# Eight weight slots made 32 bytes longer each

## The chip, the cores and the metric

The kernel runs on one core of one Trainium2 chip. The metric is the device time of one execution in microseconds; of the kernel before there are three such times, and the median counts. Engines are TensorE (PE in the profile, its weight loads PEld), VectorE (DVE), ScalarE (ACT), GpSimd (POOL) and SyncE (SP).

## The reference

For each of four batches of 6080 rows and 256 columns, q and k are divided by the norms of their columns, their 256x256 product is put through a softmax, and v is multiplied with the result. All 24320 rows then go through a feed-forward layer whose activation is a ratio of polynomials.

```python
qn = q / (np.linalg.norm(q, axis=1, keepdims=True) + 1e-06)
kn = k / (np.linalg.norm(k, axis=1, keepdims=True) + 1e-06)
s = kn.transpose(0, 2, 1) @ qn / tau
a = softmax(s)                      # along the last axis
x = (v @ a).reshape(B * N, 256)
h = x @ w_in                        # 256 -> 2048
P = a0 + a1 * h + a2 * h**2 + a3 * h**3
Q = 1.0 + abs(b0) * abs(h) + abs(b1) * h**2
out = (P / (Q + 1e-06)) @ w_out     # 2048 -> 256
```

## The kernel before

**What it computes in which order.** For each batch the 256x256 softmax is multiplied into w_in, so that h comes straight from v: h = v @ (a @ w_in). This product is made in eight pieces of 256 columns (`fuse`, line 860), one for each p from 0 to 7. Each piece is kept as two tiles whose sum is the weight: the high half `whi`, a rounded copy (fp32r) that ScalarE writes, in the tag `w`, and the rest `wlo`, which VectorE writes, in the tag `w2`. There are eight slots of each, w0 to w7 and w20 to w27, and piece p of every batch lies in slot p. They are written once for each batch.

The rows of v are taken in 48 groups, eleven of 512 rows and one of 448 for each batch. `values` (line 889) brings v with channels on the partitions and splits it in the same manner, into `vhi` and `vlo`. For each group and each p, `pair` (line 941) does this:

- first product, into the PSUM tile `hx`: two halves i of 128 columns of h. For each half there are six matmuls (`mm1`, line 958), for each of the two 128-channel parts e: whi with vhi, whi with vlo, wlo with vhi. The weights are a 128x128 block of the tile, 512 bytes on each partition, and the stream is 512 (or 448) rows of v, 2048 (or 1792) bytes. The profile calls the first and the third `hx<-vhi,w` and the second `hx<-vlo,w`: it leaves out the numbers of buffers, so both `w` and `w2` read as w.
- the rational function on ScalarE, VectorE and GpSimd, which gives its value in two parts, `gh` and `gl`;
- second product, into `acc`: for each half gh with w_out_hi, gh with w_out_lo, gl with w_out_hi, two matmuls each.

So a pair has 24 matmuls of 512 columns, with a weight load before each, and there are 384 pairs.

**What sets the order.** A planner written into the kernel puts all steps in an order by costs and due times from tables, before the program is built. Each engine then works through its own list; semaphores tell it when data are there. Addresses play no part in it.

**Where tiles lie.** The pools have one buffer for each tile, laid one behind another in the order in which the loop over `homes` (lines 1140 to 1146) makes them, each start rounded up to 32 bytes. From that follow the starts on each partition, in bytes:

| tiles | start, before | residue of 128 | residue of 512 |
|---|---|---|---|
| ones | 17024 | 0 | 128 |
| w_in, w_out_hi, w_out_lo | 17888, 34272, 50656 | 96 | 480 |
| d, uu, r, kq, sq, orow | 67040 to 128480 | 96 | 480 |
| w0 to w7 | 132832 + 2048 each | 96 | 224 |
| w20 to w27 | 149216 + 2048 each | 96 | 224 |
| vst, vhi, vlo, sacc, ssq, gh, gl | 165600 to 208608 | 96 | 224 |

The blocks of 128 columns within a tile are 512 bytes apart and the two parts e of vhi, vlo, gh and gl 2048, so they all begin at the residue of their tile.

Of the kernel before, what the change touches and what calls it, by code (L numbers as in the profile page):

```python
# [10 lines left out]
F32 = mybir.dt.float32  # L11
# [286 lines left out]
def tile_channel_attention_rational_ffn(  # L298
# [15 lines left out]
    P = 128  # L314
# [51 lines left out]
    homes = {}  # L366
# [773 lines left out]
    for tag, width in homes.items():  # L1140
        if tag in ("hA", "hB"):
            continue
        home, n = (ps, SLOTS["hA" if tag == "hx" else tag]) if tag in ("hx", "acc") else (sb, SLOTS[tag])
        if tag == "n2":
            width += 16
        homes[tag] = [home.tile([P, width], F32, name=f"{tag}{i}") for i in range(n)]
    for s in plans[0][1]:
        s.fn()
# [39 lines left out]
```

## Time and profile before

| | |
|---|---|
| three runs | 2393.72, 2396.09, 2396.17 us; median 2396.09 |
| profiled execution | 2392.04 us, of which the span from first to last instruction is 2390.1 |
| PE busy | 2333.6 us (98%), 10312 matmuls |
| PEld busy | 1936.2 us (81%) |
| DVE, ACT, POOL busy | 2151.3, 2062.4, 1836.2 us (90, 86, 77%) |
| mean granted TensorE clock | 0.992 |

Times in the rows are microseconds from the start of the span unless marked ns. A busy TensorE means that some matmul is in flight; the end of a matmul is modelled, and each overlaps the next (389 ns long, 227 ns from start to start). How fast the matmuls follow one another is therefore read from start times, or from the chain of waits, where a row gives the time that a number of them took one after another.

### The profile page before, as it was taken

The numbers are of one execution on the slowest core, as the hardware profiler recorded it, in microseconds if no ns is written. First come the engines' busy times: TensorE is split into PE (matmuls) and PEld (weight loads), VectorE is DVE, ScalarE is ACT, GpSimd is POOL, SyncE is SP. The second block draws the span as 40 slices with busy tenths as digits, with TensorE's granted clock in tenths as the row PEclk, the third lists the DMA queues.
The fourth block names the chain that finished last, engine by engine and source line by source line (L and its number), as shares of the span: only waits on it lengthen the run. The fifth ranks groups of instructions, "written<-read, shape, count | busy, mean of one in ns | idle before, by whom it ended". The sixth has DMA issues, their size and how long they took to land.

```text
span 2390.1 us, 30382 instructions
## 1 busy us (share of the span) xinstructions
PE 2333.6 (98%) x10312; PEld 1936.2 (81%) x10312; DVE 2151.3 (90%) x2627; ACT 2062.4 (86%) x2072; POOL 1836.2 (77%) x1427
## 2 busy tenths in 40 slices
PE   7899999999999999999999999999998999999998
PEld 6688888888888888888888888888887788888887
DVE  5889999997878899999987889999996999999998
ACT  4789999987767799999986789999997999999996
POOL 7798777779779977777768987777774777777775
PEclk8999999999999999999999999999999999999999
DMA  9532121136467611211136731211111121111201
GB/s 298 160 77 36 18 36 18 18 58 150 88 141 156 122 26 20 34 19 26 27 83 146 162 72 20 34 19 27 26 19 18 19 35 18 27 28 18 33 11 19
DMA packets 455862, 141.15 MB, mean 59 GB/s; under 512 B 395888, under 2 KB 445040, under 8 KB 455696
## 3 DMA queue, kind: packets, MB, share of 16 engines
q1 hardware_dynamic: 447152, 108.04, 21.9%
q0 software_dynamic: 8544, 31.07, 7.3%
q8 instruction: 83, 1.36, 0.2%
q14 instruction: 83, 0.68, 0.1%
HBM read 83.10 MB, written 24.90 MB: 45 GB/s over the span
## 4 chain that ended last, share of the span: by engine, by line
PE 67%; ACT 15%; DVE 10%; issue 5%; DMA 1%; POOL 1%; SPq 0%; DVEq 0%; POOLq 0%; ACTq 0%
PE hx L83 37%; PE acc L83 30%; ACT d L83 6%; ACT r L83 5%; DVE hx L83 4%; ACT uu L83 3%; DVE gh L83 2%; DVE orow L83 2%; DVE gl L83 1%; POOL d L83 1%; DMA r<-in_q_dram 0%; DMA out_dram<-orow 0%; ACT L83 0%; DMA kq<-in_q_dram 0%; DMA d<-in_moe_w_in_dram 0%
## 5 line engine op out<-in xcount | busy, mean ns | idle before, releaser
L83 POOL TENSOR_TENSOR d<-d,gh 128x512 f32<-128x512 f32 (+1 forms) x768 | 978.6, 1303 | 411.1 <-DVE gh L83 407.1
L83 PE MATMUL hx<-vhi,w 128*128 128x512 f32 (+1 forms) x3072 | 1045.5, 389 | 5.1 <-DVE gl L83 4.1
L83 PEld LDWEIGHTS hx<-vhi,w 128*128 128x128 f32 x3072 | 577.1, 188 | 125.6 <-DVE gl L83 8.7
L83 DVE SCALAR_TENSOR_TENSOR hx<-hx,fast,d 128x512 f32<-128x512 f32 (+1 forms) x768 | 566.4, 745 | 60.4 <-POOL d L83 59.9
L83 PE MATMUL hx<-vlo,w 128*128 128x512 f32 (+1 forms) x1536 | 595.4, 388 | 0.0
L83 ACT ACTIVATE uu<-hx,fast 128x1024 f32<-128x1024 f32 (+1 forms) x384 | 422.3, 1100 | 148.9 <-PE hx L83 148.9
L83 DVE TENSOR_TENSOR gl<-hx,r 128x512 fp32r<-128x512 f32 (+1 forms) x768 | 518.1, 678 | 31.9 <-PE acc L83 4.8
L83 POOL TENSOR_SCALAR d<-d,ones,fast 128x1024 f32<-128x1024 f32 (+1 forms) x384 | 466.2, 1217 | 93.0 <-ACT r L83 89.9
L83 DVE SCALAR_TENSOR_TENSOR gh<-hx,fast,r 128x1024 fp32r<-128x1024 f32 (+1 forms) x384 | 485.5, 1265 | 43.6 <-ACT r L83 34.2
L83 DVE SCALAR_TENSOR_TENSOR hx<-uu,fast,hx 128x1024 f32<-128x1024 f32 (+1 forms) x384 | 487.4, 1269 | 32.3 <-ACT d L83 17.3
L83 PE MATMUL acc<-gh,w_out_hi 128*128 128x512 f32 (+1 forms) x1536 | 478.7, 393 | 14.2 <-DVE orow L83 10.8
L83 PE MATMUL acc<-gl,w_out_hi 128*128 128x512 f32 (+1 forms) x1536 | 472.6, 389 | 1.8 <-DVE gl L83 1.8
L83 PE MATMUL acc<-gh,w_out_lo 128*128 128x512 f32 (+1 forms) x1536 | 470.7, 388 | 0.0
L83 ACT ACTIVATE r<-d,fast 128x1024 f32<-128x1024 f32 (+1 forms) x384 | 439.0, 1144 | 11.1
L83 ACT ACTIVATE d<-hx 128x1024 f32<-128x1024 f32 (+1 forms) x384 | 386.7, 1007 | 63.1 <-PE hx L83 54.9
L83 ACT ACTIVATE r<-r 128x1024 f32<-128x1024 f32 (+1 forms) x384 | 403.0, 1050 | 8.3
L83 ACT ACTIVATE d<-d 128x1024 f32<-128x1024 f32 (+1 forms) x384 | 403.3, 1051 | 7.1
L83 PEld LDWEIGHTS acc<-gh,w_out_hi 128*128 128x128 f32 x1536 | 285.4, 188 | 82.1 <-DVE orow L83 25.1
L83 PEld LDWEIGHTS acc<-gl,w_out_hi 128*128 128x128 f32 x1536 | 287.9, 188 | 60.8 <-DVE gl L83 3.7
L83 PEld LDWEIGHTS acc<-gh,w_out_lo 128*128 128x128 f32 x1536 | 288.3, 188 | 57.8
L83 PEld LDWEIGHTS hx<-vlo,w 128*128 128x128 f32 x1536 | 288.7, 188 | 56.6
L83 PE MATMUL hx<-kq 128*128 128x256 f32 (+1 forms) x592 | 138.1, 388 | 11.6 <-DVE fast L83 6.8
(118 smaller groups left out, 1119.3 us busy)
## 6 DMA issues: line engine op xcount, KB each, us to landing
ssq<-sq POOLq DMA_DIRECT2D x54, 512.0 KB, 5.3
vst<-in_v_dram SPq DMA_DIRECT2D x176, 128.0 KB, 4.1
out_dram<-orow SPq DMA_DIRECT2D x176, 128.0 KB, 3.3
kq<-in_k_dram SPq DMA_DIRECT2D x75, 256.0 KB, 4.1
kq<-in_q_dram SPq DMA_DIRECT2D x75, 256.0 KB, 4.6
d<-in_moe_w_in_dram SPq DMA_DIRECT2D x8, 512.0 KB, 5.2
ssq<-sq POOLq DMA_DIRECT2D x6, 448.0 KB, 5.3
r<-in_k_dram SPq DMA_DIRECT2D x9, 256.0 KB, 5.4
```

Of the source, the lines that this page charges most:

```text
L83: ins = op(*args, **kwargs)
```

## The change

The slots of the tag `w` alone are made with eight more float32 each, 2080 bytes in place of 2048, and used through a view of the first 2048. No instruction changes its operation, shape or place in the order.

```diff
         if tag == "n2":
             width += 16
+        if tag == "w":
+            homes[tag] = [home.tile([P, width + 8], F32, name=f"{tag}{i}")[:, :width] for i in range(n)]
+            continue
         homes[tag] = [home.tile([P, width], F32, name=f"{tag}{i}") for i in range(n)]
```

The starts are then:

| tiles | start, after | residue of 128 | residue of 512 |
|---|---|---|---|
| w0, w1, w2, w3 | 132832, 134912, 136992, 139072 | 96, 0, 32, 64 | 224, 256, 288, 320 |
| w4, w5, w6, w7 | 141152, 143232, 145312, 147392 | 96, 0, 32, 64 | 352, 384, 416, 448 |
| w20 to w27 | 149472 + 2048 each | 96 | 480 |
| vst, vhi, vlo, sacc, ssq, gh, gl | 165856 to 208864 | 96 | 480 |

All tiles made before w0 stay where they were; all those behind w7 lie 256 bytes further on.

## Rows read from the trace of the kernel before

**Rows 1.** Granted clock: span and mean share of TensorE's full clock.

```profile
core 0: 2390.1 us, clock 0.992
```

**Rows 2.** The page: busy time of each engine, and the chain that ended last.

```profile
PE 2333.6 (98%) x10312; PEld 1936.2 (81%) x10312; DVE 2151.3 (90%) x2627; ACT 2062.4 (86%) x2072; POOL 1836.2 (77%) x1427
...
PE 67%; ACT 15%; DVE 10%; issue 5%; DMA 1%; POOL 1%; SPq 0%; DVEq 0%; POOLq 0%; ACTq 0%
PE hx L83 37%; PE acc L83 30%; ACT d L83 6%; ACT r L83 5%; DVE hx L83 4%; ACT uu L83 3%; DVE gh L83 2%; DVE orow L83 2%; DVE gl L83 1%; POOL d L83 1%; DMA r<-in_q_dram 0%; DMA out_dram<-orow 0%; ACT L83 0%; DMA kq<-in_q_dram 0%; DMA d<-in_moe_w_in_dram 0%
```

**Rows 3.** Busy time by stretch: engines with instruction counts, granted clock, DMA share.

```profile
100.00:500.00 400.00, 395.98 (x1732) 323.75 (x1731) 376.44 (x443) 373.44 (x365) 318.39 (x242) 1.00 0.22 41
500.00:1000.00 500.00, 497.54 (x2228) 416.75 (x2227) 428.49 (x526) 402.25 (x408) 405.92 (x316) 1.00 0.44 91
1000.00:1500.00 500.00, 497.69 (x2224) 415.55 (x2223) 445.65 (x544) 423.32 (x427) 396.35 (x310) 1.00 0.36 70
```

**Rows 4.** Chain from 1000 to 1100 us: start, time, and how many matmuls.

```profile
1002.30 5.44 PE acc L83 x24
1007.74 2.73 PE hx L83 x12
```

**Rows 5.** TensorE in order of time: a float32 product of k and q.

```profile
730.50 3.61 PE L83 MATMUL hx<-kq 128*128 128x256 f32 x16
```

**Rows 6.** Groups by line: first-product loads and writers of w, busy us, mean ns.

```profile
L83 PEld LDWEIGHTS hx<-vhi,w 128*128 128x128 f32 x3072 | 577.1, 188 | 125.6 <-DVE gl L83 8.7
...
L83 PEld LDWEIGHTS hx<-vlo,w 128*128 128x128 f32 x1536 | 288.7, 188 | 56.6
...
L83 DVE TENSOR_TENSOR w<-hx,w 128x512 fp32r<-128x512 f32 x32 | 21.9, 688 | 17.1 <-ACT w L83 17.0
...
L83 ACT ACTIVATE w<-hx 128x512 fp32r<-128x512 f32 x32 | 18.9, 595 | 30.7 <-PE hx L83 26.8 <-DVE hx L83 3.9
```

**Rows 7.** TensorE around 632 and 1222 us: small matmuls, weights from ssq and from ones.

```profile
632.38 0.95 PE L83 MATMUL hx<-ones,ssq 128*128 128x1 f32 x8
...
1222.25 0.61 PE L83 MATMUL hx<-kq,ones 128*128 128x128 f32 x4
1222.61 0.45 PE L83 MATMUL acc<-gl,w_out_hi 128*128 128x448 f32 x1
```

**Rows 8.** Matmuls, then loads, around 220 us: the second load of a pair is late.

```profile
219.77 0.39 PE L83 MATMUL hx<-vlo,w 128*128 128x512 f32 x1
...
221.13 0.39 PE L83 MATMUL hx<-vlo,w 128*128 128x512 f32 x1
...
219.77 0.46 PEld L83 LDWEIGHTS hx<-vhi,w 128*128 128x128 f32 x2
...
220.45 0.41 PEld L83 LDWEIGHTS hx<-vhi,w 128*128 128x128 f32 x2
```

**Rows 9.** Loads, then matmuls, around 572 us: the same, and what follows.

```profile
571.92 0.47 PEld L83 LDWEIGHTS hx<-vhi,w 128*128 128x128 f32 x2
...
572.14 0.62 PE L83 MATMUL hx<-vhi,w 128*128 128x512 f32 x2
...
573.76 0.62 PE L83 MATMUL acc<-gh,w_out_hi 128*128 128x512 f32 x2
```

**Rows 10.** TensorE: two rows of six 448-column matmuls, and what follows the first.

```profile
615.46 0.36 PE L83 MATMUL hx<-vhi,w 128*128 128x448 f32 x1
...
616.67 0.62 PE L83 MATMUL acc<-gh,w_out_hi 128*128 128x512 f32 x2
...
618.05 0.36 PE L83 MATMUL hx<-vhi,w 128*128 128x448 f32 x1
...
634.84 0.37 PE L83 MATMUL hx<-vhi,w 128*128 128x448 f32 x1
...
636.08 0.57 PE L83 MATMUL acc<-gl,w_out_hi 128*128 128x448 f32 x2
```

## The prediction

> **What bounds the kernel now.** I read the clock of the core first, then the busy times of the page, then the same by stage, then the chain that ended last, and only then single stretches of TensorE. [...] TensorE has an instruction in flight for 2333.6 of 2390.1 us [rows 2]; the stage table shows 395.98 of 400 us, then 497.5 and 497.7 of 500 [rows 3]. A busy share says little of how tightly matmuls follow one another, so the chain is the better witness: 67% of it is TensorE, 37% on the first product (hx) and 30% on the second (acc), and ScalarE and VectorE hold another 25% [rows 2]. So a gain on TensorE reaches the end only in part (I take its share of the chain, two thirds), a loss nearly in full.
>
> The chain also gives the pace. Twenty-four second-product matmuls of 512 columns take 5.44 us, that is 226.7 ns from one to the next, and twelve first-product ones take 2.73 us, 227 ns [rows 4]. Both products run at one pace, although the eight weight tiles of the first, the streamed vhi and vlo and the second product's gh and gl were laid out in other places than w_out_hi and w_out_lo. [...]
>
> **The change part by part.** No instruction is added, removed or moved; every queue has the same rows in the same order. What differs is addresses.
>
> The eight slots w0 to w7 hold the high halves of the fused weights. All began at residue 96 of 128 bytes, as w_out, w2, vhi, vlo, gh and gl do. Now w0 and w4 stay at 96, w1 and w5 begin at 0, w2 and w6 (the slots, not the w2 tiles) at 32, w3 and w7 at 64. A 128-column block of them is 512 bytes, so every load from a slot begins at the slot's residue. Eight times 32 is 256, so all that lies behind moves by 256 bytes and keeps its residue. Before, the first product had weights and stream at the same residue of 512 (224 and 224), the second at different ones (480 and 224), and the pace was the same 227 ns [rows 4]; so I cost the move by 256 at nothing.
>
> The writers: ScalarE writes the slots 32 times in all (18.9 us) and VectorE reads them back 32 times (21.9 us) [rows 6]. Even a tenth more on both would be 4 us, beside TensorE, on engines that are idle for 240 us and more of the span [rows 2]; I take 0, with 0 to 2 us for the range.
>
> The loads: of 4608 first-product loads (3072 with vhi, 1536 with vlo) [rows 6] two in three read a w slot (the third product, with vhi, reads w2), 3072, and six slots in eight have a new residue: **2304 loads**. Their own length is shown as 188 ns [rows 6], but that is not what bounds the pace. Where one-column matmuls leave nothing else to wait for, eight of them with their loads from ssq (residue 96) take 0.95 us, 0.12 us each at most, and four matmuls with weights from ones (residue 0) give way to the next after 0.36 us with three loads in it, 0.12 us each again [rows 7]. So a load needs at most 0.12 us of a step of 0.227 us, and it begins with the step: nearly half the step is slack, at either residue. A load that became a tenth longer would still cost nothing. That is the first reason for **no change**.
>
> The second is what happens when a load comes late. At 219.77 us two loads together took 0.46 us in place of 0.41: the second waited some 50 ns for data. The matmuls went on without a trace of it: from the one at 219.77 to the one at 221.13 there are six steps in 1.36 us, 227 ns each [rows 8]. The load read its 512 bytes at quite another moment of the running matmul's stream, and the stream was not slowed. [...] Price by this row: 0.
>
> The row that speaks against it: at 571.92 us the same thing happened (0.47 us), and this time the seven steps from the matmul at 572.14 to that at 573.76 us took 1.62 us, 231 ns each, 1.62 - 7 x 0.2267 = 0.033 us lost before the pace came back [rows 9]. And where 448 columns are streamed, one and the same row of six first-product matmuls takes 1.21 us (202 ns) in one place and 1.24 us (207 ns) in another, and the six 512-column ones that follow the first take 1.38 us (230 ns) [rows 10]. So the pace has states, and the moment at which a load reads can push TensorE from the good one into a worse one for a few matmuls. [...]
>
> Bounds of the unknown price for one affected half (six matmuls): from nothing [rows 8] to 33 ns lost [rows 9]; on the other side, at most the 12 ns between the paces of rows 4 and 5 gained at each affected load. I take nothing, since the 24 and 12 matmuls of rows 4 ran at one pace with different distances between weights and stream. **Sum:** 2392.0 us for the profiled execution (span 2390.1) + 0 = 2392.0; the median of the three runs is 4.1 us above it, so 2396.1, and I forecast **2396 us**.
>
> **The rivals.** *Slower: weights out of step with the stream.* Now all weights and streams share a residue and the pace sits in its good state. If a load that begins 32, 64 or 96 bytes off acts like the late load of rows 9, each affected half is pushed out of it once. Halves: 768, six slots in eight, 576; 576 x 33 ns = 19 us if each loses that. If only the residues that differ by an odd multiple of 32 (0 and 64: four slots) do so, 384 x 33 = 12.7 us; at 4.4 ns (231 against 226.7) on each of 2304 loads, 10 us. TensorE is the bound, so nearly all reaches the end: 2406 to 2415, **2410** as its value. For it: rows 9 and 10. Against it: rows 8. It decides from 8 ns lost per half on (576 x 8 ns = 4.8 us).
>
> *Faster: the equal residue is itself what costs.* If part of the 12 ns is a clash of two reads that begin on the same residue, the 2304 matmuls lose it: at most 2304 x 12 ns = 27.6 us of TensorE, two thirds at the end, 18 us; at the 5 ns between the states of rows 10, 2304 x 5 ns x 0.67 = 7.7 us. **2388** as its value, 2378 at the far end. For it: the gap between rows 4 and 5. Against it: the float32 products have the equal residue too and pay nothing, and a late load pays as much [rows 8]. [...]
>
> *The change does nothing at all* would look like the forecast. The starts follow from the sizes (2080 bytes a slot in place of 2048), so the residues do move.
>
> **How the numbers follow.** A measurement of this kernel tells about 0.2% (4.8 us) from no change: the three runs span 2.5 us. Forecast 0.48, of it 0.46 within 0.2% and 0.01 either side. Slower rival 0.35, of it 0.03 within. Faster rival 0.17, of it 0.03 within. So faster 0.15, same 0.52, slower 0.33. For 8 in 10 the range takes the forecast, the slower rival to 2416 (all but some 0.07 of it) and the faster one to 2386 (all but some 0.08): 2386 to 2416. The forecast's own range is 2392 to 2400.
>
> **What would show it.** Right: rows of twelve first-product matmuls still at 2.72 or 2.73 us, as those of the second product; TensorE's busy time by stage within 1 us. Slower rival: first-product steps of 229 to 232 ns, with the second product's 227 disturbed only behind them, and in some slots only; the shares of ScalarE and VectorE in the chain fall. Faster: steps of 215 to 222 ns in the same slots, and more idle time of TensorE behind VectorE. What would make me wrong is a price that the trace cannot show because all its weights begin alike, above all one that holds at every load and not only for a few matmuls.

## The result, and the profile after

The changed kernel takes 2410.05 us (2409.56 to 2410.24, three runs) against 2396.09: 14.0 us more, a ratio of 1.0061 with an interval of 1.0038 to 1.0084. It is slower. The forecast of no change was wrong; the time lies inside the range and on the value of the slower rival, though, as will be seen, by two errors that cancel.

The profiled execution has a span of 2408.4 us, 18.3 more than [rows 1]'s, at a granted clock of 0.991; in the three stretches of [rows 3] it is 1.00 as before. Its page, busy time first and then the chain by engine and by line:

```profile
PE 2357.8 (98%) x10312; PEld 1937.7 (80%) x10312; DVE 2151.6 (89%) x2627; ACT 2066.7 (86%) x2072; POOL 1836.9 (76%) x1427
...
PE 89%; ACT 5%; DVE 3%; issue 2%; DMA 1%; POOL 0%; SPq 0%; DVEq 0%; POOLq 0%; ACTq 0%
PE hx L83 48%; PE acc L83 41%; ACT d L83 2%; ACT r L83 1%; DVE hx L83 1%; ACT uu L83 1%; DVE gh L83 1%; DMA kq<-in_q_dram 0%; DVE orow L83 0%; DVE gl L83 0%; DMA r<-in_q_dram 0%; POOL d L83 0%; ACT L83 0%; ACT kq L83 0%; DVE r L83 0%
```

VectorE and GpSimd did the same work in the same time, ScalarE took 4 us more over the whole. TensorE is busy 24.2 us longer with the same 10312 matmuls, and its share of the chain has gone from 67% to 89%, while that of ScalarE and VectorE together fell from 25% to 8%: part of the waits that used to lie between its stretches is now covered by its own slowness. Of 24.2 us, 18.3 reached the end of this execution; its idle time fell from 2390.1 - 2333.6 = 56.5 to 2408.4 - 2357.8 = 50.6 us.

The loads are not longer. This is their group, and the two writers of the slots (busy us, mean ns), to be held against [rows 6]:

```profile
L83 PEld LDWEIGHTS hx<-vhi,w 128*128 128x128 f32 x3072 | 577.2, 188 | 132.2 <-DVE gl L83 6.0 <-DVE w L83 1.3
...
L83 DVE TENSOR_TENSOR w<-hx,w 128x512 fp32r<-128x512 f32 x32 | 22.0, 689 | 18.4 <-ACT w L83 18.1
L83 ACT ACTIVATE w<-hx 128x512 fp32r<-128x512 f32 x32 | 19.1, 596 | 30.6 <-PE hx L83 26.7 <-DVE hx L83 3.9
```

What is longer is the step from one matmul to the next, and by slot. A pair has two sixes of first-product matmuls, and in this stretch the slots follow one another, so the chain of the changed kernel can be read slot by slot (start, time, and how many matmuls). From 1078.41 us on: the second six of slot 0, both of slots 1 and 2, the second of slot 3, the first of slot 4, then slot 4's second with slot 5's first, slot 5's second, the two of slot 6, those of slot 7, and slot 0 again.

```profile
1078.41 1.36 PE hx L83 x6
...
1080.69 1.39 PE hx L83 x6
...
1083.45 1.39 PE hx L83 x6
...
1086.66 1.40 PE hx L83 x6
...
1089.44 1.40 PE hx L83 x6
...
1094.99 1.39 PE hx L83 x6
...
1097.56 1.40 PE hx L83 x6
...
1101.68 2.80 PE hx L83 x12
...
1104.94 1.39 PE hx L83 x6
...
1109.07 2.75 PE hx L83 x12
...
1115.45 1.40 PE hx L83 x6
...
1117.31 1.40 PE hx L83 x6
...
1120.09 1.36 PE hx L83 x6
```

Only slot 0 keeps 1.36 us a six, half of the 2.73 us for twelve in [rows 4]. Slot 4, at the same residue of 128 as slot 0, does not. The table gives the mean step of the first product over the whole trace, worked out from the start times of all its 512-column matmuls (steps under 250 ns, so without waits; some 4170), each six counted to its slot by the order in which the kernel issues them. Before, that mean is 227.0 ns, and no slot is above 227.8.

| slot | 0 | 1 | 2 | 3 | 4 | 5 | 6 | 7 |
|---|---|---|---|---|---|---|---|---|
| weights' start less stream's start, of 256 bytes | 0 | 32 | 64 | 96 | 128 | 160 | 192 | 224 |
| mean step after, ns | 227.2 | 231.3 | 232.5 | 230.7 | 233.8 | 232.1 | 229.0 | 233.8 |

The mean over all slots is 231.32 ns against 227.04, 4.28 more; on the 4224 first-product matmuls of 512 columns that is 18.1 us. The second product, whose distances changed by 256 bytes alone, went from 227.04 to 228.63 ns, 6.7 us more on as many. Together 24.8 us, which is the 24.2 us of busy time within the reading. The matmuls of 448 columns take no part: their mean steps were 202.7 and 203.0 ns (steps under 222 ns) and are 202.7 and 203.3.

### The profile page after: what moved, and what is told of

Same layout as the page of the kernel before. It is cut to its first block, busy times and chain, and to the rows that moved or that the text cites. A ratio compares the mean times of both kernels' runs of the same rounds, so it can differ in the third digit from the quotient of the medians.

```text
span 2408.4 us, 30382 instructions
## 1 busy us (share of the span) xinstructions
PE 2357.8 (98%) x10312; PEld 1937.7 (80%) x10312; DVE 2151.6 (89%) x2627; ACT 2066.7 (86%) x2072; POOL 1836.9 (76%) x1427
## 3 DMA queue, kind: packets, MB, share of 16 engines
q8 instruction: 83, 1.36, 0.2%
## 4 chain that ended last, share of the span: by engine, by line
PE 89%; ACT 5%; DVE 3%; issue 2%; DMA 1%; POOL 0%; SPq 0%; DVEq 0%; POOLq 0%; ACTq 0%
PE hx L83 48%; PE acc L83 41%; ACT d L83 2%; ACT r L83 1%; DVE hx L83 1%; ACT uu L83 1%; DVE gh L83 1%; DMA kq<-in_q_dram 0%; DVE orow L83 0%; DVE gl L83 0%; DMA r<-in_q_dram 0%; POOL d L83 0%; ACT L83 0%; ACT kq L83 0%; DVE r L83 0%
## 5 line engine op out<-in xcount | busy, mean ns | idle before, releaser
L83 PE MATMUL hx<-vhi,w 128*128 128x512 f32 (+1 forms) x3072 | 1057.9, 393 | 3.6 <-DVE gl L83 2.7
L83 PEld LDWEIGHTS acc<-gh,w_out_hi 128*128 128x128 f32 x1536 | 285.3, 188 | 78.0 <-DVE orow L83 17.5
```

The lines of the kernel that those rows point to most:

```text
L83: ins = op(*args, **kwargs)
```

## The experiments

Three theories had to be told apart. Below, weights or a load are called off, or at an odd distance, when their start is no multiple of 256 bytes from that of the stream. **D**: a matmul is slowed when the weights that are loaded while it runs lie at a distance from its stream that is no multiple of 256 bytes. **R**: what counts is the residue of the weights' own start. **L**: any new layout behind the slots costs something. In all kernels below the instructions and their order are those of before; a table of extra words for single tiles moves what lies behind them, and each tile is used through a view of its old width:

```diff
+    PADS = {...}                 # extra float32 at the end of (tag, number)
-        homes[tag] = [home.tile([P, width], F32, name=f"{tag}{i}") for i in range(n)]
+        homes[tag] = [home.tile([P, width + PADS.get((tag, i), 0)], F32, name=f"{tag}{i}")[:, :width] for i in range(n)]
```

sm1 is the last tile ahead of w0. The lines quoted under each run are rows of its chain (start, time, count) unless said otherwise.

**All behind moved by 256.**

```diff
+    PADS = {("sm", 1): 64}
```

> The eight slots keep their 2048 bytes; one small tile ahead of w0 is 256 bytes longer, so w0 and all that lies behind it move by 256 bytes together. Theory D (what counts is the distance between the weights being loaded and the rows being streamed, and distances of a multiple of 256 cost nothing): hx distance 0, acc distance 0 instead of 256, steps of 227 ns in both, 2396 us within 5. Theory R (what counts is the residue of the weights' own start): no residue of 256 changes, 2396 within 5. Theory L (any new layout behind w costs about what the change cost): 2405 to 2415.

2394.48 us against 2395.52 of before in the same session, ratio 0.9999 (0.9989 to 1.0009).

```profile
1004.07 5.44 PE acc L83 x24
1009.51 2.73 PE hx L83 x12
```

These are the paces of [rows 4]. L falls, and the side effect of the change, large tiles lying 256 bytes further on, costs nothing (here the slots move too), as the prediction had it.

**All eight slots moved by 128, their residue of 128 kept.**

```diff
+    PADS = {("sm", 1): 32, ("w", 7): 32}
```

> All eight w slots begin 128 bytes later, all at residue 96 of 128 as before; w2 and all behind keep a multiple of 256. Theory D with a period of 256: every slot is now where slot 4 was in the changed kernel, whose halves lost 43 ns; 768 halves x 43 = 33 us and a third more behind them in acc, 44 us on TensorE, of which about 0.7 reaches the end: 2427, within 2415 to 2440; hx steps of 232 to 237 ns. Theory D or R with a period of 128 bytes, as the change's own words have it: 2396 within 5, hx steps 227.

2417.64 us, ratio 1.0092 (1.0075 to 1.0109): 22.1 us more.

```profile
1014.56 5.45 PE acc L83 x24
1020.01 2.81 PE hx L83 x12
```

The period is not 128 bytes. The mean step of the first product is 234.2 ns, what slot 4 had (233.8), so the loss of 43 ns a half was right; the time came out below the expected 2427 and inside its bounds. Little of the loss went on into acc (227.8 ns, not a third more): TensorE lost some 33 us, not 44.

**No weights moved, only the stream.**

```diff
+    PADS = {("w2", 7): 32, ("vlo", 1): 32}
```

> No weight tile moves at all: vst, vhi and vlo alone begin 128 bytes later, everything behind vlo 256. Theory D: all six loads of a half lie 128 off the stream, so hx steps of 232 to 240 ns and 2415 to 2440 us, acc 227 once it has settled. Theory R (the weights' own start): nothing has changed for any load, 2396 within 5.

2412.99 us, ratio 1.0073 (1.0056 to 1.0090): 17.5 us more.

```profile
1013.36 5.44 PE acc L83 x24
1018.81 2.79 PE hx L83 x12
```

Every weight tile lies where it lay, w0 to w27 at their old addresses, and the first product is slow (mean step 232.1 ns). R falls by this run alone. That it is the pair of addresses, and not the start of the stream for itself, the next run shows. The time is just under the expected 2415.

**Weights and stream moved together.**

```diff
+    PADS = {("sm", 1): 32}
```

> All from w0 on begins 128 bytes later: w, w2, vhi, vlo together, gh and gl too, while w_out stays. Theory D: the first product has distance 0 again and keeps 227 ns, the second has 128 between w_out and gh, gl and takes the loss, 232 to 237 ns on 4608 matmuls, 2415 to 2440 us. Theory R: the first product's weights are at another residue of 256, hx slow and acc at 227, 2415 to 2440 us. So the time is the same by both, and the product that is slow tells them apart.

2418.72 us, ratio 1.0094 (1.0077 to 1.0110): 23.2 us more, and the slow product has changed places.

```profile
1015.56 5.59 PE acc L83 x24
...
1025.30 2.73 PE hx L83 x12
```

The second product, whose gh and gl moved and whose w_out stayed, has gone from 5.44 to 5.59 us for 24, a mean step of 233.0 ns. The first product keeps 2.73 us where it runs for itself; its mean of 228.8 ns is raised by the steps next to acc (232.3 for the last of a six before acc, whose running time covers acc's first load, and 230.9 for the first after acc). So distance it is, in both products.

**All slots moved by 192.**

```diff
+    PADS = {("sm", 1): 48, ("w", 7): 16}
```

> All eight w slots begin 192 bytes later, 64 short of the next multiple of 256 from the stream; all else as in the run with 256 behind. It is the distance that slot 6 had in the changed kernel, whose halves lost 14 ns, the least of all. Theory D (distance between weights and stream, period 256): 768 halves x 14 = 11 us and a third more in acc, 14 us on TensorE, two thirds of it at the end: 2405, within 2400 to 2411. If slot 6 was only lucky in what ran before it, the loss is that of 128 bytes: 2415 to 2420. If any distance but 0 can beat 227 ns, this is the likeliest: below 2390.

2401.89 us, ratio 1.0032 (1.0022 to 1.0042): 7.3 us more, inside the expected 2400 to 2411. The mean step is 229.3 ns, slot 6's in the changed kernel (229.0). Slot 6 was not lucky; 192 is the cheapest distance that was tried, and still dearer than 0.

```profile
1008.05 5.46 PE acc L83 x24
1013.51 2.75 PE hx L83 x12
```

**Only the other set of weights moved by 128.**

```diff
+    PADS = {("w", 7): 32, ("w2", 7): 32}
```

> Only the slots of the other set, w2, begin 128 bytes later; w, vhi, vlo keep distance 0 or 256. Two of a half's six loads are off in place of four. Theory D with a price for each load: half of what the run with w off by 128 lost (22 us), 2407, within 2402 to 2412. Theory D with a price for each change between the two distances (whi, whi, wlo, whi, whi, wlo: as many changes as before): about the same 2418. If the loads of wlo were hidden, 2396.

2404.71 us, ratio 1.0043 (1.0026 to 1.0060): 10.1 us more, near the price for each load (11 us) and far from the price for each change of distance (22). A fixed price for each load does not hold beyond this pair of runs, though. A half here, with two of its six loads off, loses 6 x (231.14 - 227.04) = 25 ns, one with four off 43 (all slots by 128), but one with all six off only 6 x (232.13 - 227.04) = 31 (the stream moved). The chain, and then one six of TensorE in order of time (start, us, count):

```profile
1006.07 5.44 PE acc L83 x24
1011.52 2.77 PE hx L83 x12
```

```profile
1074.97 0.39 PE L83 MATMUL hx<-vhi,w 128*128 128x512 f32 x1
1075.20 0.40 PE L83 MATMUL hx<-vlo,w 128*128 128x512 f32 x1
1075.43 0.62 PE L83 MATMUL hx<-vhi,w 128*128 128x512 f32 x2
1075.89 0.40 PE L83 MATMUL hx<-vlo,w 128*128 128x512 f32 x1
1076.13 0.40 PE L83 MATMUL hx<-vhi,w 128*128 128x512 f32 x1
1076.36 0.62 PE L83 MATMUL acc<-gl,w_out_hi 128*128 128x512 f32 x2
```

The six take 1076.36 - 1074.97 = 1.39 us in place of 1.36.

In the order of mm1 the third and sixth matmuls read w2. A load begins with the matmul before the one that it serves (before, at the median 3 ns after that matmul's start; here the third's load at 1075.20 us, as the second matmul), so these loads run during the second and fifth. Worked out from all start times, the six steps of a half have means of 226.9, 232.5, 233.9, 227.2, 232.3 and 234.1 ns, and the same pattern stands, to 2 ns at each step, in 601 of 704 halves. The first slow step is that of the matmul at 1075.20, whose own weights lie at a good distance; the load that runs beside it, of weights at an odd one, is what differs. The next is that of the matmul that uses the odd weights, whose neighbour load is a good one again. Then the pace is back at 227. One odd load thus costs 12 ns on two steps.

The first of the two steps could also be long because the next matmul, with its odd weights, starts late. The last second-product matmul before a first product tells these apart (mean of some 530 steps, 227.2 ns before). With only the stream moved, the load beside it lies well to its stream and only the next matmul's own weights lie badly: 227.5 ns. With all slots moved by 128 the load beside it is off: 232.5 ns. So it is the load that slows the matmul beside which it runs. The second slow step is its after-effect: with the stream moved, the first matmul of the second product follows a load that was off, while its own weights and the next load lie well to its stream, and it still takes 231.6 ns in place of 227.1.

**Every large tile begins 32 bytes later.**

```diff
-    fast = const.tile([P, 16], F32, name="fast")
+    fast = const.tile([P, 24], F32, name="fast")
```

> One constant ahead of w_in is 32 bytes longer, so every large tile (w_in, w_out, d to orow, w, w2, vhi, vlo, gh, gl) begins 32 bytes later, at a multiple of 128. All distances stay what they were. Theory D: 227 ns in both products, 2396 within 5. [...]

2393.97 us against 2394.58, ratio 0.9996 (0.9986 to 1.0006).

```profile
1003.94 5.44 PE acc L83 x24
1009.38 2.73 PE hx L83 x12
```

With all starts at multiples of 256 in place of residue 224 nothing changes: 5.44 and 2.73 us, 227 ns a step in both products, as in [rows 4]. The start of the stream for itself, 96 bytes into 128 or at a multiple of 128, makes no difference here.

**All from kq on moved by 128.**

```diff
+    PADS = {("r", 2): 32}
```

> All from kq on begins 128 bytes later, w_in, w_out, d, uu and r stay. The second product is 128 off as in the run that moved all from w0, so 2415 to 2422 us and acc steps near 233 ns. What is asked of it is the float32 product of the fused weights: its weights lie in kq, its stream in w_in, and they are now 128 apart in place of 0. Theory D for every product: its steps of 216 ns grow by 4 ns or more. [...]

2416.95 us in one run, inside the expected 2415 to 2422. The second product is slow as in the run that moved all from w0 (233.0 ns a step). The float32 product of the fused weights, in order of time; first a stretch of this run, then the like of the kernel before:

```profile
662.72 3.72 PE L83 MATMUL hx<-w_in_sb,kq 128*128 128x256 f32 x16
```

```profile
654.56 3.72 PE L83 MATMUL hx<-w_in_sb,kq 128*128 128x256 f32 x16
```

The second product's row for 24 is this:

```profile
1013.02 5.57 PE acc L83 x24
```

Sixteen instructions take 3.72 us at a distance of 128 as at 0, and over the whole trace the mean step of this product is 215.8 ns against 215.7. Theory D for every product, which asked for 4 ns or more, falls. This float32 product, 0.84 ns a column (215.8 ns for 256), does not feel the distance of 128; the two fp32r products, 0.44 ns a column before (227.0 ns for 512), do (234.2 and 233.0 ns at 128).

**All slots moved by 32, and by 224.**

```diff
+    PADS = {("sm", 1): 8, ("w", 7): 56}
```

> All eight w slots begin 32 bytes later than a multiple of 256 from the stream, the distance that slot 1 had in the changed kernel, whose halves lost 28 ns in hx. Theory D with one price for each distance: hx steps of 227 + 28 / 6 = 231.7 ns, 768 x 28 = 21.5 us on TensorE and some more in acc; the two uniform runs so far had 43 and 14 ns a half and came out 22 and 7 us later, so about 14 us later, 2408 to 2410. If the price in the changed kernel came from the mixture of slots, another value: below 2404 or above 2414.

```diff
+    PADS = {("sm", 1): 56, ("w", 7): 8}
```

> All eight w slots begin 32 bytes short of a multiple of 256 from the stream, the distance that slot 7 had in the changed kernel, whose halves lost 42 ns. Theory D with one price for each distance: hx steps of 234 ns, as with 128, 21 us later, 2413 to 2419; so 32 bytes to one side cost more than 32 to the other. If distance counted by size alone, the same as the run with 32: 2408 to 2410.

2416.37 us, ratio 1.0089 (1.0072 to 1.0106), and 2422.29, ratio 1.0117 (1.0100 to 1.0134), against 2394.41. First the chain of the run with 32, then of that with 224:

```profile
1016.89 5.45 PE acc L83 x24
1022.34 2.78 PE hx L83 x12
```

```profile
1013.52 5.47 PE acc L83 x24
1018.99 2.80 PE hx L83 x12
```

The steps of the first product are as expected, 231.9 and 233.6 ns (slots 1 and 7: 231.3 and 233.8), so in the first product each distance has its own price, mixed or not. Both times were missed, 2408 to 2410 and 2413 to 2419 being too low; by its time alone the run with 32 would have spoken for the mixture, which was to show above 2414. The steps say where the error is: in what follows the slow six. There acc stands at 229.8 and 229.5 ns, against 227.8 after 128 and 227.1 after 192. Why the second product takes longer to find its pace after some distances than after others is not shown. 32 and 224 bytes are the same size of distance to either side, and their price differs by 6 us.

The change and the six runs with a slow first product can be put beside one another. TensorE's loss is 4224 matmuls of 512 columns times the sum by which both mean steps exceed 227.04 ns, the mean of either before (those of 448 columns stay within 2 ns of theirs in every run and are left out); the times are against before in the same session, and the share is the time over the loss.

| kernel | hx step, ns | acc step, ns | lost on TensorE, us | later, us | share |
|---|---|---|---|---|---|
| the change | 231.32 | 228.63 | 24.8 | 14.0 | 0.56 |
| w + 192 | 229.29 | 227.12 | 9.8 | 7.3 | 0.74 |
| w2 + 128 | 231.14 | 227.02 | 17.2 | 10.1 | 0.59 |
| stream + 128 | 232.13 | 228.45 | 27.5 | 17.5 | 0.64 |
| w + 32 | 231.91 | 229.81 | 32.3 | 22.0 | 0.68 |
| w + 128 | 234.18 | 227.75 | 33.2 | 22.1 | 0.67 |
| w + 224 | 233.56 | 229.52 | 38.0 | 27.9 | 0.73 |

The change's own share is the least certain: its interval of 1.0038 to 1.0084 is 9 to 20 us, so 0.4 to 0.8. All in all some two thirds of TensorE's loss reaches the end.

## Why the prediction was wrong, point by point

**The bound was read rightly** (TensorE held 67% of the chain before and 89% after), and so was what the change touches: where the weights begin. That the move of everything behind the slots costs nothing held (the run with 256), the writers cost 0.2 and 0.1 us, and the loads kept their 188 ns.

**The step that failed** is "I take nothing, since the 24 and 12 matmuls of rows 4 ran at one pace with different distances between weights and stream". The two distances that the kernel before has are 0 in the first product and 256 in the second. They differ only when counted within 512 bytes; by the runs both are multiples of 256 and cost the same, nothing. The one tile at another residue of 128, ones, is met in small products alone [rows 7], so the trace held no row that could price any other distance for the fp32r products; I took the absence of a contrast for the absence of a price. The term put at nothing measured 24.8 us on TensorE, 18.1 in the first product and 6.7 in the second, and 14.0 us at the end. The prediction names this in its last sentence as what would make it wrong, and gave it too little weight.

**The slack of the load** (rows 7) was true and beside the point. The load has time to spare and is not lengthened (188 ns before and after); the matmul beside it is slowed (a mean step of 231.32 ns in the first product against 227.04).

**Late loads.** Of two late loads one left no trace [rows 8] and one lost 33 ns [rows 9], and I took the price from the first. A load that comes late shifts the moment, the change shifts the address, and only the second was at issue. What rows 9 showed, that TensorE can be pushed out of its pace by a load and needs more than one step to return, is what the runs with a distance show as well: two slow steps after one odd load, and in four of the seven kernels of the table a second product of 228.4 to 229.8 ns. It was the row to go by.

**The slower rival** gave 2410 and 2410 it is, but not by its own sum. Its sums gave 10 to 19 us on TensorE (576 halves at 33 ns at the top), nearly all of it at the end. It left slot 4 out, whose residue of 128 had not changed; with a period of 256 slot 4 is among the dearest (233.8 ns a step), and seven slots in eight are hit. Their 616 halves of 512 columns lost 18.1 us in the first product, 29 ns each, and 6.7 us more were lost in the second. Against that, not nearly all reached the end but 0.56 by the medians, 0.59 to 0.74 in the runs (18.3 of 24.2 us between the two profiled executions): the waits between TensorE's stretches shrank. The loss was sized too small and the share too large, and that the two meet at 2410 is luck. (Its threshold of 576 x 8 ns is 4.6 us, not 4.8; nothing hangs on it.)

**The faster rival** has no ground left. No distance that was tried, seven in the slots of the changed kernel and four of them for all slots, gives a first product under 227 ns, and neither does another start of the stream (2.73 us for twelve in the run with every large tile 32 bytes later). Its sum takes 12 ns a load, the step of rows 4 less that of rows 5, (3.61 - 0.39) / 15 = 215 ns with 0.39 us for the last instruction alone. The one is a step of 512 fp32r columns and the other of 256 float32 columns; no run shows that the first can come down to the second, so the 12 ns were an estimate, and what the runs showed in their place is 227 ns at best. That the float32 products pay nothing, which I put down against a clash of two reads, was no argument: the one that was tried at a distance of 128 does not feel that either (215.8 ns a step against 215.7).

## What to carry to other kernels

Where fp32r matmuls bound a kernel and weights are loaded beside a running stream, try the starts of weights and stream a multiple of 256 bytes apart: here that kept 227 ns for a step of 512 columns, and every other distance that was tried cost 2 to 7 ns of it. Slots that lay 32 bytes off made the kernel 22.0 us longer. Before a price is set to nothing, see whether the trace holds a contrast in that very quantity: a kernel in which all starts share a residue cannot show what a residue costs. And a loss on the bounding engine need not all be paid at the end: here, where other engines and issue still held a third of the chain before, about two thirds of it were.

## What the runs showed that I had not expected

The price is not even in the distance: 229 ns a step at 192, 232 at 32, 234 at 128 and 224. The pace of 227 ns is a state that the matmuls fall back into, not a sum of parts: one odd load in three gives 227, 232, 234 and 227 again in most halves, and six odd loads in six (31 ns a half) cost less than four (43 ns). What in TensorE or in its memory makes the period 256 bytes, and why a step of 512 fp32r columns takes 227 ns even at the best distance where one of 256 float32 columns takes 215.7, stays open: neither another distance nor another start brought it down. Making each slot 256 bytes longer in place of 32, which by these runs should keep the distance at a multiple of 256, was not tried.
